# A two-branch layer (state-space scan and gated FFN) on one core: a new order of all queues, earlier gate and phases, lane swap by DMA, and dummy matmuls first

## The chip, the cores and the metric

The kernel runs on one core of one Trainium2 chip. The metric is the device time of the kernel in microseconds (us). The profiled span, from the first to the last instruction, is about 1.7 us shorter than the time. Five engines matter: TensorE (PE, the matmuls; PEld its weight loads), VectorE (DVE), ScalarE (ACT), GpSimd (POOL) and the queue engine SP, which issues most of the DMA transfers. Each engine works through its own instructions in program order and waits on semaphores for the others. PSUM is the memory that the matmuls write, divided into banks; an eviction is the copy of a finished bank to another memory, and the bank can be written again only after it. The granted clock is the share of its full speed that TensorE was given.

## The reference, cut to what matters

```python
# x: (1, 2048, 448) bf16;  P = D = 448;  F = 1792
g = sigmoid((x * gate_w).sum(-1, keepdims=True))           # one number per row
# branch a: diagonal complex state space
Lam_bar = exp(dt * Lam);  B_bar = ((Lam_bar - 1) / Lam)[:, None] * B
h[t] = Lam_bar * h[t-1] + B_bar @ x[t]                      # 2048 steps
a = 2 * real(C @ h) + x * Dskip
# branch b: FFN
b = silu(x @ w1) @ w2
out = g * a + (1 - g) * b
```

## The kernel before

Two time steps are folded into one, so the scan has 1024 steps. `XT` holds x transposed, its even and odd rows one above the other. The parts that count here:

- `ffn1(c, fb)`: 4 matmuls of 512 columns, evicted by ScalarE with silu. There are four passes `c` of 14 blocks. `ffn2(c, q)`: 14 matmuls of 448 columns, evicted by ScalarE with the gate as scale.
- `bu(m, h)`: 7 matmuls of 512 columns for the scan's input, row block `m` of 8, evicted by ScalarE into `HS`.
- tables: the scan is done in a rotating frame. For each of 4 lane groups VectorE computes a phase (3 operations of 128x1024) and ScalarE makes sine and cosine of it.
- `scan(pt)`: VectorE rotates, runs the recurrence, and rotates back into `HS`.
- `ytile`: 8 matmuls `HS` x `C` plus 4 for the direct part; VectorE mixes it with the FFN result. `k0`: 28 matmuls for the direct part, from `CO`.
- The last lane group has only 64 complex lanes. They are packed, real parts in the upper and imaginary parts in the lower half of block 6. A rotation needs the other half as well, so the kernel computes block 7, the same lanes swapped, by matmul.

Their order before (cut; `side` is a generator of VectorE and ScalarE work, `pump` runs a piece of it):

```python
side = chain(side_params(), side_tables(0), side_coef(), side_diag(), side_C(True),
             side_tables(1), side_gate(), side_tables(2), side_tables(3), side_C(False))
for _ in range(2):
    next(side)                      # parameters and tables(0) stand AHEAD of all FFN1
for c in range(2):
    for fb in range(NFB):
        ffn1(c, fb)
        pump()                      # tables 1..3 and the gate between FFN1's evictions
for pt in range(3):
    ...                             # bu of two blocks, then scan(pt)
... bu(6), bu(7), rest of side, scan(3), k0
ffn2(0) x4; ffn1(2); ffn2(1) x4; ffn1(3); ffn2(2) x4
ffn2(3, q), ytile, store ...

def side_tables(pt):
    X, RR = G[:, 0, :], G[:, 1, :]  # ONE shared buffer: phase pt+1 waits for ScalarE's tables of pt
    ...
def side_gate():
    for kt in range(NKT):
        s = kt % 2
        ld("sp", OT[s][:, :], x2[kt * 128:(kt + 1) * 128, :], f"OT{s}_0")   # two small buffers
        ...                         # two products with row sums
```

## Time and profile before

| | before |
|---|---|
| time, median of 3 runs | 215.34 us (214.61 to 218.18) |
| profiled span | 213.8 us |
| PE busy | 163.9 us (77%) |
| DVE busy | 114.1 us (53%) |
| mean granted TensorE clock | 0.894 |

A run more than 1.5% above the fastest of its kernel, as 218.18 us is here, counts as slow.

The first view is the page's second part for the kernel before: the span in 40 equal slices of 5.3 us, each digit the busy share in tenths; PEclk is the granted TensorE clock.

```profile
...
PE   0550009939703349999999999999999999999994
...
DVE  0439999903567696499999999700000021213332
...
PEclk9997556975985557999999999999999999999999
...
```

From slice 16 (about 80 us) PE is full to the end. Ahead of that it holds little work and, having been idle, drops to half clock (the fives). So the loss lies in the first 80 us.

The second view is the list of waits of PE in the kernel before (who waited for whom: total us, times, longest), and the third the timeline of PE (start, length, what, and in brackets the idle time ahead of it with what ended it).

```profile
...
PE ps L493 <- ACT AT L498: 37.9, 5, 17.6
...
```

```profile
...
12.23 1.89 PE L493 MATMUL ps<-XT,W1E 128*128 128x512 bf16 x8 [0.51 <-DMA W1E<-in_B_w_dram]
31.68 11.47 PE L493 MATMUL ps<-XT,W1E 128*128 128x512 bf16 x43 [17.55 <-ACT AT L498]
46.81 10.70 PE L493 MATMUL ps<-XT,W1E 128*128 128x512 bf16 x35 [3.66 <-ACT AT L498]
66.51 1.89 PE L493 MATMUL ps<-XT,W1E 128*128 128x512 bf16 x4 [9.01 <-ACT AT L498]
72.66 1.89 PE L493 MATMUL ps<-XT,W1E 128*128 128x512 bf16 x4 [4.26 <-ACT AT L498]
77.93 3.59 PE L493 MATMUL ps<-XT,W1E 128*128 128x512 bf16 x8 [3.39 <-ACT AT L498]
81.32 18.98 PE L528 MATMUL ps<-XT,LT 128*128 128x512 bf16 x81
```

PE waits 37.9 us for `AT` evictions: four PSUM banks are full, and ScalarE, whose queue is in order, is itself standing at a sine table. What it stands for shows in the chain of waits (start, length, what), a piece of it:

```profile
...
61.90 2.50 DMA OT<-in_A_x_dram
...
67.67 1.24 DVE G L380
...
68.94 1.06 ACT SIN L382
...
76.25 1.15 ACT COS L385
77.39 0.49 ACT AT L498
...
77.93 3.59 PE ps L493 x8
81.53 7.12 PE ps L528 x29
...
```

Gate load, gate, phase, sine, absolute value, cosine, the next phase, its tables, and only then an FFN1 eviction, 8 last FFN1 matmuls at half clock (3.59 us, 449 ns each), and Bu.

### The profile page before, as it was taken

The page shows a single profiled execution, that of the slowest core. Times are in us where ns is not written, and L with a number is a line of the kernel's source. Part 1 is how long each engine was busy: PE and PEld are TensorE (multiplying, and loading weights), DVE is VectorE, ACT ScalarE, POOL GpSimd, SP SyncE. Part 2 cuts the span into 40 slices and gives each one's busy share as a digit, 9 for nine tenths or more (in the row PEclk, how much of TensorE's full clock was granted, in tenths as well). Part 3 has the DMA queues.
Part 4 walks back from the last instruction along what each step waited for, and adds up shares of the span by engine and source line. Part 5 has one row for each costly group of instructions (what it writes and reads, how often), then busy time and mean ns, then how long its engine had stood idle before and what let it go on. Part 6 is the DMA issues. An engine that isn't in the chain of part 4 may idle for free.

```text
span 213.8 us, 2064 instructions
## 1 busy us (share of the span) xinstructions
PE 163.9 (77%) x784; PEld 77.2 (36%) x792; DVE 114.1 (53%) x212; ACT 71.3 (33%) x112; POOL 7.3 (3%) x16
## 2 busy tenths in 40 slices
PE   0550009939703349999999999999999999999994
PEld 0210003403300013444455544454445555555552
DVE  0439999903567696499999999700000021213332
ACT  0500095393102682434332277325642201110000
POOL 7500000000000000000000000000000000000000
PEclk9997556975985557999999999999999999999999
DMA  6998498795440000000000000000000001111111
GB/s 141 351 295 156 88 168 156 209 335 210 129 129 2 0 0 0 0 0 2 3 0 0 0 3 0 0 0 0 3 0 0 0 3 43 43 43 46 43 55 73
DMA packets 27363, 14.58 MB, mean 68 GB/s; under 512 B 20885, under 2 KB 26458, under 8 KB 27354
## 3 DMA queue, kind: packets, MB, share of 16 engines
q1 hardware_dynamic: 26384, 12.85, 23.5%
q10 hardware_dynamic: 970, 1.61, 2.2%
q8 instruction: 6, 0.10, 0.2%
q14 instruction: 3, 0.02, 0.0%
HBM read 8.03 MB, written 1.84 MB: 46 GB/s over the span
## 4 chain that ended last, share of the span: by engine, by line
PE 62%; DVE 15%; DMA 11%; SPq 7%; ACT 3%; issue 1%; DVEq 0%
PE ps L511 20%; PE ps L493 13%; PE ps L528 12%; PE ps L610 11%; DMA OT<-in_A_x_dram 8%; SPq L208 4%; SPq L205 3%; DVE JK L457 3%; PE ps L621 3%; DMA Y<-in_A_B_re_dram 3%; PE ps L543 3%; DVE TMP L340 2%; DVE BB L342 2%; DVE G L380 2%; ACT COS L385 1%
## 5 line engine op out<-in xcount | busy, mean ns | idle before, releaser
L493 PE MATMUL ps<-XT,W1E 128*128 128x512 bf16 x110 | 34.8, 482 | 38.5 <-ACT AT L498 37.9
L629 DVE SCALAR_TENSOR_TENSOR OT<-ps,GT,LT 128x448 bf16<-128x448 f32 x16 | 10.9, 684 | 62.5 <-PE ps L621 54.3
L511 PE MATMUL ps<-W,AT 128*128 128x448 bf16 x224 | 43.4, 352 | 0.0
L498 ACT ACTIVATE AT<-ps 128x512 bf16<-128x512 f32 x56 | 32.4, 596 | 15.6 <-PE ps L493 15.6
L493 PEld LDWEIGHTS ps<-XT,W1E 128*128 128x128 bf16 x112 | 12.5, 117 | 59.9 <-ACT AT L498 42.0
L511 PEld LDWEIGHTS ps<-W,AT 128*128 128x128 bf16 x224 | 21.7, 98 | 20.0 <-issue 0.2
L528 PE MATMUL ps<-XT,LT 128*128 128x512 bf16 x110 | 25.1, 389 | 0.1
L516 ACT ACTIVATE LT<-ps,GT 128x448 bf16<-128x448 f32 x16 | 10.1, 633 | 44.5 <-PE ps L511 44.5
L493 PE MATMUL ps<-XT,W1O 128*128 128x512 bf16 x108 | 24.0, 379 | 0.2
L457 DVE SCALAR_TENSOR_TENSOR JK<-OT,GWB 128x448 bf16<-128x448 bf16 x16 | 10.0, 625 | 12.5 <-DMA OT<-in_A_x_dram 11.9
L528 PEld LDWEIGHTS ps<-XT,LT 128*128 128x128 bf16 x112 | 11.3, 101 | 14.2 <-issue 1.7
L564 DVE TENSOR_TENSOR_SCAN G<-P,Q 128x1024 f32<-128x1024 f32 x7 | 15.7, 2278 | 0.0
L493 PEld LDWEIGHTS ps<-XT,W1O 128*128 128x128 bf16 x112 | 11.0, 98 | 13.1
L532 ACT ACTIVATE HS<-ps 128x512 bf16<-128x512 f32 x16 | 9.6, 597 | 15.5 <-PE ps L528 15.5
L610 PE MATMUL ps<-CE,HS 128*128 128x448 bf16 x64 | 13.4, 352 | 0.0
L610 PE MATMUL ps<-CO,HS 128*128 128x448 bf16 x64 | 13.4, 352 | 0.0
L382 ACT ACTIVATE SIN<-G 128x1024 bf16<-128x1024 f32 x4 | 4.2, 1056 | 22.4 <-DVE G L380 22.4
L610 PEld LDWEIGHTS ps<-CO,HS 128*128 128x128 bf16 x64 | 6.3, 98 | 5.8
L610 PEld LDWEIGHTS ps<-CE,HS 128*128 128x128 bf16 x64 | 6.1, 98 | 5.1
L340 DVE TENSOR_SCALAR TMP<-XC,P 128x448 f32<-128x448 bf16 x16 | 7.2, 453 | 0.5
L621 PE MATMUL ps<-KT,XT 128*128 128x448 bf16 x32 | 7.4, 352 | 0.0
L561 DVE TENSOR_TENSOR Q<-G,SIN 128x1024 bf16<-128x1024 f32 x6 | 7.3, 1219 | 0.0
(69 smaller groups left out, 112.0 us busy)
## 6 DMA issues: line engine op xcount, KB each, us to landing
OT<-in_A_x_dram SPq DMA_DIRECT2D x8, 224.0 KB, 2.5
out_dram<-OT SPq DMA_DIRECT2D x8, 224.0 KB, 1.9
W<-in_B_w_dram SPq DMA_DIRECT2D x1, 1568.0 KB, 8.2
W1O<-in_B_w_dram SPq DMA_DIRECT2D x1, 1344.0 KB, 10.7
W1E<-in_B_w_dram ACTq DMA_DIRECT2D x1, 1152.0 KB, 7.1
W1E<-in_B_w_dram ACTq DMA_DIRECT2D x2, 192.0 KB, 5.8
BB<-in_A_B_re_dram SPq DMA_DIRECT2D x1, 336.0 KB, 6.8
BB<-in_A_B_im_dram SPq DMA_DIRECT2D x1, 336.0 KB, 7.1
```

The lines of the kernel that those rows point to most:

```text
L340: T.op("dve", lambda e: e.tensor_scalar(TMP[:, :], y, ys, None, ALU.mult), reads=reads, writes=["TMP"])
L457: T.op("dve", lambda e, s=s, i=i, kt=kt: e.scalar_tensor_tensor(JK[:, :], OT[s][:, i * D:(i + 1) * D], 1.0, GWB[:, i * D:(i + 1) * D], ALU ...
L493: ins = pe.matmul(ps[:, bank, :], W[:, j, fb * 128:(fb + 1) * 128], XT[:, j0 + j, h * 512:(h + 1) * 512], start=(j == 0), stop=(j == 3))
L498: T.op("act", lambda e: e.activation(a[:, fb, :], ps[:, bank, :], AF.Silu), reads=[f"ps{bank}"], writes=[f"AT{c % 2}_{fb}"])
L511: ins = pe.matmul(ps[:, bank, 0:D], a[:, fb, q * 128:(q + 1) * 128], W2[:, fb, :], start=(fb == 0), stop=(fb == NFB - 1))
L516: T.op("act", lambda e: e.activation(bs(tile), ps[:, bank, 0:D], AF.Copy, scale=GT[:, 2, tile:tile + 1]), reads=[f"ps{bank}", "GT2"], writ ...
L528: ins = pe.matmul(ps[:, bank, :], LT[:, m, j, :], XT[:, j, h * 512:(h + 1) * 512], start=(j == 0), stop=(j == 6))
L532: T.op("act", lambda e: e.activation(HS[:, m, 8 + h * 512:8 + (h + 1) * 512], ps[:, bank, :], AF.Copy), reads=[f"ps{bank}"], writes=[f"U{m ...
L564: T.op("dve", lambda e: e.tensor_tensor_scan(G[:, c, :], rb, Q1[:, c, :], 0.0, ALU.mult, ALU.add), reads=[f"Q1{c}", "rr"], writes=[f"G{c}"])
L610: ins = pe.matmul(ps[:, bank, 0:D], HS[:, m, o0:o0 + 128], C[:, m, :], start=(m == 0), stop=False)
L621: ins = pe.matmul(ps[:, bank, 0:D], XT[:, j, t0:t0 + 128], KT[:, j, :], start=False, stop=(j == 3))
L629: T.op("dve", lambda e: e.scalar_tensor_tensor(o[:, odd * D:(odd + 1) * D], ps[:, bank, 0:D], GT[:, 1, tile:tile + 1], bs(tile), ALU.mult, ...
```

## The change

Intent: give PE work from the first microseconds on and put everything of VectorE and ScalarE next to it. Its parts:

1. Order of PE: FFN1 pass 0, Bu of blocks 0, 1, 6, FFN1 pass 1, Bu of 2 to 5, then FFN2 and FFN1 by turns, k0, y. ScalarE's tables are put between evictions at chosen places.
2. Phases of all four groups are computed early, each into the part of `HS` that its Bu product fills later, so no phase waits for a table. The gate comes before the scans, from one load of x into the still unused `W1O`.
3. The swapped lanes are made by DMA (a swap of halves of `HS` before and of a product after the scan), so `bu(7)` and the eighth products of y go.
4. Twelve dummy matmuls ahead of the first real one, to raise the clock.
5. Smaller: lincombs in pairs through two temporaries, activation tables loaded ahead, FFN2, Bu, k0 and y share four PSUM banks.

```diff
+        def warm(n):                       # n matmuls of zeros into a bank nobody reads
+            ...
+        warm(9)
+        T.op("pe", mm_cols, ...)
+        warm(3)
 ...
+        def phase(pt):
+            return HS[:, 2 * pt:2 * pt + 2, :].rearrange("p a b -> p (a b)")[:, 0:2 * NK].bitcast(F32)
 ...
+        XN = W1O[:, :, :].rearrange("p a b -> p (a b)")
+        def load_xn():
+            ld("sp", XN.rearrange("p (k c) -> p k c", k=NKT), x2.rearrange("(k p) c -> p k c", p=128), "XN")
 ...
+                T.dma("sp", lambda e: e.dma_start(u[0:64, 1, :], u[64:128, 0, :]), ...)     # scan(3)
+                T.dma("sp", lambda e: e.dma_start(u[64:128, 1, :], u[0:64, 0, :]), ...)
 ...
+                T.dma("sp", lambda e: e.dma_start(Q2[0:64, 1, :], Q2[64:128, 0, :]), ...)
+                T.dma("sp", lambda e: e.dma_start(Q2[64:128, 1, :], Q2[0:64, 0, :]), ...)
 ...
-                for m in range(8):         # ytile
+                for m in range(7):
 ...
+        for fb in range(NFB):
+            ffn1(0, fb)
+            if fb in (8, 10, 12):
+                run(tabs, 1)               # tables of groups 0 and 3
+        for h in range(2):
+            for c in range(2):
+                bu(c, h)
+                run(tabs, 1)
+        bu(6, 0)
+        bu(6, 1)
+        load_w2()
+        run(gates, 5)
+        s3 = scan(3)
+        run(s3, 1)
+        for fb in range(NFB):
+            ffn1(1, fb)
+            if fb % 3 == 2:
+                run(tabs, 1)               # tables of groups 1 and 2
+        run(gates)
+        run(s3, 1)
+        run(coef, 1)
+        run(s3)
+        load_c()
+        run(scan(0))
+        ... bu(2), bu(3), scan(1), bu(4), bu(5), scan(2)
+        ... ffn2(0), ffn1(2), ffn2(1), run(coef) (diagonals, CO, CE), ffn1(3), ffn2(2), k0
```

## The prediction

> **What bounds the kernel now.** Span 213.8 us (time 215.3, 1.5 more). In the stretch table TensorE (PE) is at 99% from 80 us to the end at clock 1.00, but holds only 31 us of work in the first 80. The chain of waits says why: through 81 us it runs over VectorE (DVE) and queue issues, not PE. B combinations wait for their last load until 14.7; PE's first FFN1 half then waits for evictions that stand behind ScalarE's sine tables, and those behind DVE's phases (PE idle 17.6 us before 31.7, then 3.7); the gate's x loads come through two buffers (9.4 us, then about 2.5 each); the last tables run one at a time (66 to 77). Idle PE also falls to clock 0.50 (427 instead of 216 ns per 512-column matmul).
>
> From 81.5 on everything is PE work. So all PE work at full clock is: FFN1 224x0.2165 = 48.5, Bu 112x0.2165 = 24.2, FFN2 42.4, k0 5.6, y 24.2+6.1+1.5: about 153 us. About 60 us are lost, nearly all before 81.
>
> **What the change does.** PE work: lane swap by DMA removes one of eight Bu and one of eight y products: -3.0 and -3.0, leaving about 147. Order: FFN1 waits for no table; phases go to unused HS space; gate loads come as one transfer; Bu alternates with FFN1; the tables fill ScalarE gaps. Dummy matmuls (12x0.43, before the data) pay the half-clock start: the trace's first 8 real matmuls took 432 ns, the next 8 236. The Trainium skill, "TensorE: Matmul & The Clock Gate", Part 1, states full rate after about 3.4 us busy; 8.3 to 12 us here agrees.
>
> DVE gets no slack: work is 114 us, about 4 less without CE7, CO7 and BB copies' waits. Added: copies, one 0.69 add, one less 1.2 product.
>
> **PE schedule I expect:** FFN1 starts 8.5 to 9 (loads), first half ends 22; Bu0,1,6 to 31; FFN1 to 43; Bu2-5 to 55; FFN2/FFN1/FFN2/FFN1/FFN2 to 111; k0 to 117; then 39.4 (trace: 6.63 and 3.98 per tile pair, less 0.38) to 156; last eviction and store 3: span 159 unstalled.
>
> **DVE schedule:** parameters to 9.6, B and phases to about 28.6; idle until the 1.8 MB x load (issued about 27, W2 took 8.2 us for 1.6 MB) at 35; gate 10.7 to 46; scan 3 and coefficients to 56; swap wait; three scans of 14.2 to 100-103; diagonals, CO to 112, CE to 120. y needs CE at about 119, k0 needs CO at 111: DVE and PE finish nearly together, so each DVE delay after 28 us shows one for one. I expect scan 3's second swap to stand behind the 1.6 MB W1O load (10.7 us landing before) on the same queue, costing DVE some 3 us; "DMA: Bandwidth & Descriptors", on HWDGE ordering, states ring order per engine; no trace here shows it yet. With 1 to 2 us of start stalls: span about 162.5, time **164.0 us**, 8 in 10 between **158.5 and 174.0**. Faster by over 2%: 0.98; within: 0.01; slower: 0.01.
>
> **What would show it.** PE busy at least 9 tenths in nearly every slice from 9 us; Bu matmuls 216 ns; no wait of FFN1 for evictions above 2 us; DVE idle about 6 us before the gate, about 3 before scan 3's last add; k0 or first y waiting on CO/CE 0 to 4 us.
>
> **What would make it wrong.** Start loads in a new order contending (FFN1 starting after 11); x landing after 38, so that Tanh blocks Bu evictions and everything slips; DVE finishing CE past 125; PE clock lost at an early gap.

## The result, and the profile after

| | before | after |
|---|---|---|
| time, median | 214.98 us (4 runs) | 164.28 us (163.36 to 164.53, 4 runs) |
| ratio, fast runs | | 0.764 (95%: 0.760 to 0.768) |
| profiled span | 213.8 us | 162.8 us |
| PE busy | 163.9 us (77%) | 154.5 us (95%) |
| DVE busy | 114.1 us | 109.8 us |
| mean granted clock | 0.894 | 0.977 |

A ratio here is the mean time of one kernel's fast runs over that of the other's of the same rounds, so it is not quite the ratio of the medians. The forecast was 164.0 us.

The same slices (now 4.1 us each) for the kernel after:

```profile
...
PE   6549999999999999999999999999999999999992
...
DVE  0559999306999999999999999999401131133342
...
PEclk9955999999999999999999999999999999999999
...
```

PE is full from the fourth slice on; its first real work begins in the third, at 10.2 us, and what the first two hold are the dummies. The clock stands at half in slices 3 and 4, in spite of those dummies. VectorE, nearly as full as PE from slice 4 to slice 28, has one empty slice there, the ninth: its wait for the x load. The chain of waits of the kernel after is nearly PE alone; its first large pieces and the first of the y phase:

```profile
...
2.66 7.29 DMA W1E<-in_B_w_dram
...
10.20 14.85 PE ps L530 x56
25.05 9.06 PE ps L564 x42
34.11 12.09 PE ps L530 x56
46.20 12.09 PE ps L564 x56
58.29 10.59 PE ps L548 x56
...
103.93 10.59 PE ps L548 x56
114.53 1.32 PE ps L579 x7
...
120.14 2.75 PE ps L548 x14
...
```

Before 10.20 us it is queue issues and one load, the first FFN1 weights. The first pass of 56 FFN1 matmuls takes 14.85 us, the second 12.09: 2.76 us lost to half clock. Everything else is at full clock without a gap: 2x10.59 us for 112 matmuls of 448 columns is 189 ns each.

The waits of PE, and then those of DVE, in the kernel after:

```profile
...
PE ps L530 <- DMA W1E<-in_B_w_dram: 3.3, 1, 3.3
...
```

```profile
...
DVE JK L487 <- DMA W1O<-in_A_x_dram: 8.2, 1, 8.2
...
DVE HS L597 <- DMA Q<-Q: 0.2, 1, 0.2
```

The 37.9 us of waits for evictions are gone. VectorE waits 8.2 us for the one large x load, and 0.2 us for the swap. Two lines of VectorE's timeline show how early `CO` and `CE` are ready (the last instruction of each):

```profile
...
108.36 0.69 DVE L378 SCALAR_TENSOR_TENSOR CO<-XC,P,TMP 128x448 bf16<-128x448 bf16 x1
...
115.19 0.68 DVE L378 SCALAR_TENSOR_TENSOR CE<-XC,P,TMP 128x448 bf16<-128x448 bf16 x1
```

`CO` is done at 109.05 and k0 starts at 114.53; `CE` is done at 115.87 and y needs it at 122.9. So by this reading VectorE has 5.5 and 7 us in hand, where the prediction gave it none. About half of the difference is PE being late and not VectorE being early: the prediction had k0 at 111 and y at 119.

Where did 51 us go? The span falls by 51.0. Of PE's waits for evictions 37.9 us vanished; PE's busy time fell by 9.4 us, of which the trace gives 6.06 to the products that went (14 of 512 and 16 of 448 columns at 216.5 and 189 ns); the rest of it, with the dummies added, is less time at half clock. The remaining 3.7 us are mostly an earlier start: PE's waits ahead of its first work and weights were 8.0 + 0.5 us and are 1.3 + 0.6 + 3.3.

### The profile page after: what moved, and what is told of

It reads as the page before. It is cut to its first block, busy times and chain, and to the rows that moved or that the text cites. A ratio compares the mean times of both kernels' runs of the same rounds, so it can differ in the third digit from the quotient of the medians.

```text
span 162.8 us, 2017 instructions
## 1 busy us (share of the span) xinstructions
PE 154.5 (95%) x774; PEld 74.4 (46%) x774; DVE 109.8 (67%) x216; ACT 67.8 (42%) x111; POOL 7.3 (4%) x16
## 4 chain that ended last, share of the span: by engine, by line
PE 92%; DMA 4%; ACTq 1%; DVE 0%; issue 0%
PE ps L530 31%; PE ps L548 26%; PE ps L659 13%; PE ps L564 13%; DMA W1E<-in_B_w_dram 4%; PE ps L670 4%; PE ps L579 3%; ACTq L204 1%; PE ps L666 1%; DVE OT L678 0%; PE ps L662 0%; PE ps L581 0%; PE ps L464 0%
## 5 line engine op out<-in xcount | busy, mean ns | idle before, releaser
L535 ACT ACTIVATE AT<-ps 128x512 bf16<-128x512 f32 x56 | 32.7, 597 | 15.8 <-PE ps L530 15.7
L530 PE MATMUL ps<-XT,W1E 128*128 128x512 bf16 x112 | 27.1, 407 | 3.3 <-DMA W1E<-in_B_w_dram 3.3
L564 PE MATMUL ps<-XT,LT 128*128 128x512 bf16 x98 | 21.5, 379 | 0.0
L530 PEld LDWEIGHTS ps<-XT,W1E 128*128 128x128 bf16 x112 | 11.5, 103 | 18.8 <-issue 7.3
L600 DVE TENSOR_TENSOR_SCAN G<-P,Q 128x1024 f32<-128x1024 f32 x7 | 15.7, 2277 | 0.0
L564 PEld LDWEIGHTS ps<-XT,LT 128*128 128x128 bf16 x98 | 9.6, 98 | 11.6
L487 DVE SCALAR_TENSOR_TENSOR JK<-W1O,GWB 128x448 bf16<-128x448 bf16 x16 | 8.8, 622 | 8.2 <-DMA W1O<-in_A_x_dram 8.2
L659 PE MATMUL ps<-CO,HS 128*128 128x448 bf16 x56 | 11.9, 352 | 0.0
L659 PE MATMUL ps<-CE,HS 128*128 128x448 bf16 x56 | 11.9, 352 | 0.0
L568 ACT ACTIVATE HS<-ps 128x512 bf16<-128x512 f32 x14 | 8.4, 598 | 6.8 <-PE ps L564 6.6
L597 DVE TENSOR_TENSOR Q<-G,SIN 128x1024 bf16<-128x1024 f32 x7 | 8.5, 1218 | 0.0
L597 DVE TENSOR_TENSOR Q<-G,COS 128x1024 bf16<-128x1024 f32 x7 | 8.5, 1209 | 0.0
L266 PE MATMUL ps<-Q 128*128 128x512 bf16 x12 | 4.8, 569 | 1.3 <-DVE SG L211 1.3
```

The lines of the kernel that those rows point to most:

```text
L487: T.op("dve", lambda e, t=t: e.scalar_tensor_tensor(JK[:, t % 2, :], XN[:, t * D:(t + 1) * D], 1.0, GWB[:, :], ALU.mult, ALU.mult, accum_o ...
L530: ins = pe.matmul(ps[:, bank, :], W[:, j, fb * 128:(fb + 1) * 128], XT[:, j0 + j, h * 512:(h + 1) * 512], start=(j == 0), stop=(j == 3))
L535: T.op("act", lambda e: e.activation(a[:, fb, :], ps[:, bank, :], AF.Silu), reads=[f"ps{bank}"], writes=[f"AT{c % 2}_{fb}"])
L564: ins = pe.matmul(ps[:, bank, :], LT[:, m, j, :], XT[:, j, h * 512:(h + 1) * 512], start=(j == 0), stop=(j == 6))
L568: T.op("act", lambda e: e.activation(HS[:, m, 8 + h * 512:8 + (h + 1) * 512], ps[:, bank, :], AF.Copy), reads=[f"ps{bank}", f"F{pt}"], wri ...
L597: T.op("dve", lambda e: e.tensor_tensor(o, a, b, op), reads=reads, writes=writes)
```

## The experiments

Runs that were sent together shared one chip. The control, run with the first three, gave 163.55 us, ratio 0.7588. Its first FFN1 matmul started at 9.80 us, and its first FFN1 pass took 13.8 us. Experiments e4 to e6 with e8, and e7 with e9 to e11, ran on two other chips, so they are compared with the control by the ratio to the kernel before.

```profile
...
5.40 1.46 PE L266 MATMUL ps<-Q 128*128 128x512 bf16 x3
9.80 13.93 PE L530 MATMUL ps<-XT,W1E 128*128 128x512 bf16 x55 [2.94 <-DMA W1E<-in_B_w_dram]
23.57 9.23 PE L564 MATMUL ps<-XT,LT 128*128 128x512 bf16 x41
...
```

> The changed kernel itself, as the control on the same chip as the next three. Expected 163.4 to 164.6 us, first FFN1 matmul at about 10.2 us, the clock granted at 0.5 from about 8.7 to 15.5, first FFN1 half 14.9 us.

Start and clock vary from run to run by themselves: between this run and the profile above the start differs by 0.4 us and the first pass by 1 us, and the six runs of the control show mean clocks from 0.976 to 1.0. So the first pass of one profile is not a measure by itself to better than 1 us. Nor is a mean clock of 1.0 proof of full clock: the views are made of the clock changes that the trace records, and ahead of the first of these they show 1.00. In e1 the first recorded change is a rise at 14.15 us, and up to there the matmuls start 0.43 us apart, after it 0.22.

### e1: no dummies

```diff
-        warm(9)
         T.op("pe", mm_cols, ...)
-        warm(3)
```

> All 12 dummy matmuls taken out. Theory A (the dummies do nothing here: the 3.3 us without a matmul before the first weights land lose the clock again): same time as the control within 0.7 us, first FFN1 half again about 14 to 15 us. Rival (they shorten the slow start as the change intends): the first half takes longer than the control's by 1 to 2 us and so does the whole.

Measured: 163.74 us, ratio 0.7597 against 0.7588 of the control; the means of the fast runs are 163.76 and 163.51, so 0.15% apart and within the scatter. The PE timeline of this run:

```profile
...
9.66 14.45 PE L528 MATMUL ps<-XT,W1E 128*128 128x512 bf16 x55 [3.54 <-DMA W1E<-in_B_w_dram]
23.94 9.23 PE L562 MATMUL ps<-XT,LT 128*128 128x512 bf16 x41
...
```

The first pass takes 14.3 us here. As shipped, the dummies are worth nothing that shows. Theory A holds so far as that; why is for the next run.

### e2: dummies up to the data

```diff
-        warm(3)
+        warm(18)
```

> 18 instead of 3 dummies behind the parameter columns, so that they reach to about 10 us, where the first weights land. Theory A: the clock stays at 1.0, the first FFN1 half takes 12.1 us instead of 14.9, and the time falls by 2.3 to 2.9 us to about 161.6. Rival (the half rate comes from something else, such as the load of weights or a fixed start phase): no gain, or up to 0.5 us lost since the dummies overrun the data.

Measured: 161.97 us (161.75 to 162.22), ratio 0.7512, clock 1.0 in every run; its mean is 1.6 us or 1.0% below the control's. PE timeline:

```profile
...
5.04 4.06 PE L266 MATMUL ps<-Q 128*128 128x512 bf16 x18
10.28 12.27 PE L530 MATMUL ps<-XT,W1E 128*128 128x512 bf16 x55 [1.18 <-DMA W1E<-in_B_w_dram]
22.38 9.43 PE L564 MATMUL ps<-XT,LT 128*128 128x512 bf16 x41
...
```

The idle gap ahead of the data is 1.2 us instead of 2.9 to 3.3, and the pass takes 12.1 us. So reaching nearly to the data is worth 1.6 us. The run changes two things at once, the gap and the number of dummies, and the recorded clock changes suggest that both count. Twelve dummies are only just enough to raise the clock: it rose at 5.26 us in the profile after and at 6.78 in the control, and not before 13.29 in e3, which has the same twelve. Where it rose, it fell again at 8.67 and 10.19, within the gap or at its end. Here it rose at 4.02 and stayed. What in the gap decides is taken up under e11. The gain is 1.6 and not 2.3 to 2.9, because the control's own first pass lost only 1.7 us to half clock in its profiled run (13.8 against 12.1), and the data came 0.5 us later here. This version beats both kernels.

### e3: a smaller first block of weights

```diff
-        ld("act", W1E[:, 0:3, 0:512], ...); ld("act", W1E[:, 0:3, 512:], ...)
+        for k, a, b in (("W1Eb", 0, 256), ("W1Ed", 256, 768), ("W1Ec", 768, F_FF)):
+            ld("act", W1E[:, 0:3, a:b], ...)
```

> The first block of FFN1 weights cut from 512 to 256 columns (then 512, then the rest). If the first FFN1 matmul waits only for bytes ahead of it in the queue, it starts 1.0 to 1.6 us earlier (about 8.8 us) and the gap shrinks to 1.9 us. Theory A then also predicts that the clock is held or nearly so: time 160.5 to 163. If the gap is still long enough to lose the clock, only the earlier start is gained: about 163.

Measured: 163.13 us, ratio 0.7571: same as the control within the scatter. The load of half the bytes took as long (192 KB landed 7.1 us after issue; the 384 KB of the control took 6.9), and the first FFN1 matmul started at 9.98. The theory of bytes ahead in the queue fell for this load. The gap was 2.5 us and the first pass took 13.7; this run can't tell whether such a gap loses the clock, since here the dummies had not raised it.

### e4: the lanes by matmul again

```diff
-        (two swaps by DMA in scan(3))
+                tt(HS[:, 6, H0:], G[:, 0, :], cs, ...); tt(HS[:, 7, H0:], G[:, 0, :], sn, ...)
-                for m in range(7):   # ytile
+                for m in range(8):
+            bu(7, h) after bu(6, h);  LT7, C7 and their coefficients as before the change
```

> The lane swap put back on the matmul engine inside the new order (an eighth Bu product, an eighth y product, an eighth C pair, no swap by DMA). Theory (after 10 us only the sum of matmul work counts): 14 matmuls of 512 and 16 of 448 columns return, +3.0 and +3.0 us: 169.0 to 170.2 us. Rival (the swap by DMA costs nearly as much in waits as it saves): 164 to 167.

Measured: 170.65 us, ratio 0.7919, that is 7.1 us over the control if both ratios are taken of 215.3. Of it, 6.06 us are the matmuls; the trace shows 0.81 us more, a wait of the small diagonal product for a ScalarE eviction, since two more Bu products shift the rotation of the banks. The swap by DMA gives back what it takes off PE and costs nothing that shows.

### e5 and e6: VectorE delayed

```diff
         load_c()
+        for _ in range(3):     # e6: range(8); 1.22 us each, result unused
+            T.op("dve", lambda e: e.tensor_tensor(G[:, 1, :], IOTA[:, :], IOTA[:, :], ALU.subtract), ...)
         run(scan(0))
```

> Three idle 1.22 us products (3.7 us) on VectorE before the first scan. The recorded prediction said VectorE and the matmul engine finish nearly together, so each delay shows one for one: +3.7, about 167.5. The trace of the changed kernel says CO is ready 5.4 us before k0 needs it and CE 6.8 us before y: +0, about 163.6.

> Eight such products (9.8 us). One for one: about 173.4. With the slack of 5.4 us before k0 read from the trace: +4.3, about 168 (k0 then waits for CO).

Measured: e5 164.3 us, ratio 0.7621, and PE waits for nothing but its first weights; its interval (0.7586 to 0.7656) holds the control's 0.7588. 3.7 us of delay are free to within the scatter (0.7 us), and the one-for-one claim is refuted. e6 took 171.01 us, ratio 0.7934, 7.4 us over the control, where the slack read off k0 said 4.3. Its PE waits and timeline:

```profile
...
PE ps L548 <- DVE PV L468: 5.5, 1, 5.5
...
```

```profile
...
102.09 2.81 PE L548 MATMUL ps<-W,AT 128*128 128x448 bf16 x14
110.38 10.45 PE L548 MATMUL ps<-W,AT 128*128 128x448 bf16 x42 [5.47 <-DVE PV L468]
120.66 1.49 PE L579 MATMUL ps<-CO,BB 128*128 128x448 bf16 x7
...
```

The wait came up at another place: not at k0, but in the third FFN2, which needs a PSUM bank that VectorE's copy of the diagonals (`PV`, line 468) still holds. The bank was wanted at 104.9 and the copy came at 110.2. The real slack is thus about 4.3 us (9.8 minus 5.5), at that copy. And the idle 5.5 us cost the clock once more: the 42 matmuls after it took 10.28 us up to the start of k0, where 42x0.189 = 7.94 is the full rate. Wait 5.5 plus clock 2.3 makes the 7.4 with a little to spare.

### e7: the gate through two buffers again

```diff
-        load_xn()                                    # one load of 1.8 MB
+                if t % 2 == 0:
+                    ld("sp", OT[(t // 2) % 2][:, :], x2[...], ...)   # 8 loads of 224 KB, two buffers
-        load_w2()
         run(gates, 5); s3 = scan(3); run(s3, 1)
+        load_w2()
```

> The changed kernel with its gate loads through two small buffers again, as in the kernel before, at the new early place. Theory (VectorE has about 4 us of slack after the gate and waits 8 us for the one large load anyway): gate starts earlier, about 32, ends about 47 as now; time within 1 us of the control's 163.6. Rival (the single load is part of the gain): the two-buffer waits of about 2.5 us per pair and the swap standing behind them cost over 2 us.

Measured: 163.18 us, ratio 0.7562: nothing lost. VectorE's waits in it:

```profile
...
DVE JK L490 <- DMA OT<-in_A_x_dram: 5.6, 5, 1.4
...
```

The single load of the change is not part of the gain that shows: the gate starts at 31.8 instead of 38.1 and ends its last product at 45.2 instead of 46.8. Load size was not what the gate needed; that its early place was is not shown by a run of its own. This run also tells about the swap (its first two transfers of 128 KB): with no large load just ahead of them in the queue they took 2.7 us to land; in the kernel after, behind W2 of 1.6 MB, 6.8 us.

### e8 and e9: the order alone, in the kernel before

e8 takes the kernel before and changes only the place of its calls; e9 mends one spot of e8.

```diff
+        for fb in range(NFB): ffn1(0, fb)
+        pump(12)                              # params, tables(0), coefficients, diagonals, CO
+        for fb in range(NFB): ffn1(1, fb)
+        # e8: pump(1) (tables(1)); all bu; rest of side; four scans; k0; then as before
+        # e9: tables(1..3) ahead of the gate, one each ahead of Bu of 0-1, 2-3, 4-5; bu 6, 7;
+        #     rest of side; four scans; k0 only after the third FFN2
```

> The kernel before with nothing but its order changed: first FFN1 half before any table, then the first tables, the second half, all Bu, then gate, tables and scans on VectorE beside FFN2 and FFN1; no dummies, lanes by matmul, gate loads through two buffers, phases in the shared buffer. Theory (the 60 us lost were PE waiting in program order behind a VectorE chain that itself could run beside later matmul work): VectorE ends its scans at about 133, y starts at 134, end near 177: time 175 to 182, so about 37 of the 51 us. Rival (the early gate and phases are what matters, order alone is held by VectorE all the same): over 195.

> The order alone again, with the spot mended that the first such run showed (k0's evictions behind the last tables on ScalarE, 10 us of idle PE and then half clock): all tables before the gate, between the Bu groups, and k0 after the third FFN2. Nothing else of the change. Expected: Bu ends about 68, FFN2 may wait 2 to 5 us for the gate, y starts near 137, end near 178: 176 to 184 us. If it stays above 187, order alone gives only half of the 51 us and the early phases and gate are needed for the rest.

Measured: e8 191.05 us, ratio 0.8883, outside the expected 175 to 182 and below the rival's 195. Its trace shows PE idle for 9.9 us at k0, whose evictions I had put behind the last two tables in ScalarE's queue, and half clock after it. e9 gave 182.17 us, ratio 0.8436, inside the expected 176 to 184. PE timeline of e9:

```profile
...
30.68 11.63 PE L493 MATMUL ps<-XT,W1E 128*128 128x512 bf16 x39 [3.93 <-ACT AT L498]
...
47.33 6.20 PE L528 MATMUL ps<-XT,LT 128*128 128x512 bf16 x27 [2.00 <-ACT HS L532]
54.76 6.22 PE L528 MATMUL ps<-XT,LT 128*128 128x512 bf16 x28 [1.22 <-ACT HS L532]
62.20 9.24 PE L528 MATMUL ps<-XT,LT 128*128 128x512 bf16 x41 [1.22 <-ACT HS L532]
71.27 10.76 PE L511 MATMUL ps<-W,AT 128*128 128x448 bf16 x56
...
```

So order alone is worth 33.7 us of 215.6 (1 minus 0.8436), about two thirds of the gain; e8 and e9 differ by 9 us through the place of a few calls. What e9 still lacks against the kernel after (182.2 against about 163.6) is 18.6 us. Experiment e4 gives 6 to 7 us of that to the lanes. The waits that e9's timeline shows for ScalarE, 3.93 + 2.00 + 1.22 + 1.22 = 8.4 us, are those that early phases in their own memory take away; some 2.6 us of half clock follow the first of them (11.5 us from 30.68 to Bu at 42.15 for 41 matmuls, of which two records are missing; 41x0.2165 is 8.9). The profiled runs alone differ by 15.9 us (178.7 against 162.8): 6.06 + 8.4 + 2.6, less 1.4 for e9's first FFN1 matmul, at 8.79 instead of 10.20, makes 15.7. That this remainder is due to the phases is read off the trace and was not tested by a run with the phases alone.

### e10 and e11: trying to start earlier

e10: ten dummies behind the columns, meant to reach the data (they ended 2.1 us short), and the tail row block of the weights cut to its first 512 columns as well. e11: the same, and B's two loads moved behind the weights.

```diff
+        warm(10)                                           # instead of 3
-        ld("act", W1E[0:64, 3, :], B_w1[384:448, :], "W1Ea")
+        ld("act", W1E[0:64, 3, 0:512], B_w1[384:448, 0:512], "W1Ea")
+        ...                                                # the other 1280 columns after the first block
 e11:
-        ld("sp", BB[...], A_B_re...); ld("sp", BB[...], A_B_im...)
+        ld("act", BB[...], A_B_re...); ld("act", BB[...], A_B_im...)   # after all W1E loads
```

> Dummies up to the data (10 behind the columns) and the fourth row block of the FFN1 weights also cut to its first 512 columns (160 KB fewer ahead of the first product). If the load that ends last is held by bytes ahead of it in its queue, the first FFN1 matmul starts 0.5 to 1.2 us earlier than 10.2 and the time is 160.8 to 161.6; the run with dummies alone was 162.0. If the engines are simply shared with the other queue, 161.6 to 162.3.

> As the run before, and the two loads of B move from the other queue to stand behind the FFN1 weights. If the early matmul is held by sharing the engines with B (0.67 MB), it starts at 8.3 to 9.3 and the time is 160 to 161; B lands about 2 us later, which VectorE's 8 us wait before the gate should swallow. If VectorE's later start shows after all, no gain or a loss of up to 2 us.

Measured: e10 169.63 us (0.7838), 5.4 us slower than the control by the ratios, and slow in all its runs (167.9 to 171.0); two of its six were over 1.5% above the fastest, so they are left out of the ratio. e11 164.17 us (0.7618; one slow run of six, 167.82, left out), no gain. PE timelines of e10, then e11:

```profile
...
10.23 3.61 PE L531 MATMUL ps<-XT,W1E 128*128 128x512 bf16 x16 [2.10 <-DMA W1E<-in_B_w_dram]
19.54 10.64 PE L531 MATMUL ps<-XT,W1E 128*128 128x512 bf16 x39 [5.70 <-issue]
...
```

```profile
...
5.08 2.33 PE L267 MATMUL ps<-Q 128*128 128x512 bf16 x10
9.82 13.07 PE L531 MATMUL ps<-XT,W1E 128*128 128x512 bf16 x51 [2.41 <-DMA W1E<-in_B_w_dram]
...
```

Neither start moved: 10.23 and 9.82. In e10 the rest of the weights landed 15.6 us after issue instead of 10.2 (control), so PE stopped for 5.7 us after four blocks; the transposing loads of x took longer too (median 7.3 us to landing, against 5.1), but so they did in e11 (7.1). Why the same bytes, cut in two, slow the whole start phase down is open: e11 has the same cut, and its weights landed after 10.7 us. So the cut alone does not do it. What holds the first weights at 9.6 to 10.0 us is open as well; three ways of taking bytes off did not move it. e11 has a side result: its gap after the dummies was 2.4 us, and the clock was still lost (0.50 from 12 to 14 us in the stretch table, while the first matmuls after the gap ran at full rate).

That leads to what in a gap loses the clock. Its length alone does not decide: e11's 2.4 us lost it, and the 2.1 us of e10 with the same 19 dummies and the 2.34 us that e8's PE waits ahead of 46.92 did not. In all 14 traces the recorded clock changes are multiples of 3.41 us apart. Cut each trace at that step from its first change: every stretch of 3.41 us that began at full clock and in which PE was idle for 2.13 us or more ended with the fall to half (e11's from 7.69 to 11.10 holds 2.13), and every one with 1.86 us or less of idle time kept the full clock (e10's gap falls into two stretches, with 1.5 and 0.6 us; e8's likewise, with 0.97 and 1.37; e2's lies in one, with 1.18). This is read from the traces kept, with no run made to test it.

## Why the prediction was right or wrong, point by point

The forecast, 164.0 us, met 164.28. Part of this is luck: two terms of the sum were off and cancelled, the half clock (2.8 us instead of none) and the wait for VectorE (none instead of about 2).

- "About 60 us are lost, nearly all before 81", and the sum of PE work near 147 us: right. The chain after shows 149.5 us of PE from 10.20 to 159.67, of which 2.76 are half clock, so 146.7 of work. The largest part of the gain is order (e9: 33.7 us).
- "Lane swap by DMA removes ... -3.0 and -3.0": right (e4: +7.1, of which 6.06 matmuls and 0.81 a bank wait).
- "Dummy matmuls pay the half-clock start": this step failed. I took the Trainium skill's "TensorE: Matmul & The Clock Gate", Part 1, for the rise of the clock and left out of the sum that it need not last over the gap to the data, although I placed that data at 8.5 to 9 us and had only 12x0.43 = 5.2 us of dummies; "PE clock lost at an early gap" stands only in the list of what would make the prediction wrong. The same page's section "HAM oscillation" warns of idle gaps over about 3.4 us; the gap here was 3.3 us in the profile after and 2.9 in the control, so that figure would not have warned me. e1 (no dummies: no change) and e2 (dummies nearly to the data: -1.6 us) settle that the step failed. The term was 2.76 us in the profiled run.
- "FFN1 starts 8.5 to 9", with 1 to 2 us for start stalls: it started at 10.2, so it fits only with that allowance used up.
- "Each DVE delay after 28 us shows one for one", CE at 120, k0 or y waiting 0 to 4 us: this step failed. CE was ready at 115.9 and nothing waited. I had costed lincombs (linear combinations, two VectorE operations each) at about 1.14 us; in pairs they take 0.96 (1.91 a pair in the timeline after, against 1.21 for a single one before), and the 16 gate products, which now write two buffers by turns, 0.55 instead of 0.67 (that the buffers are the cause was not tested). The other part is PE: it came to k0 and to y 3.5 and 3.9 us later than planned. e5 shows 3.7 us of delay to be free; e6 puts the slack at about 4.3 us, held by a PSUM bank and not by CO or CE.
- "Scan 3's second swap ... costing DVE some 3 us": wrong in size, 0.2 us. The swap did stand behind another load (6.8 us for the first swap against 2.7 in e7), which fits "DMA: Bandwidth & Descriptors", on HWDGE ordering (of the DMAs that SP and ScalarE issue: descriptors of one engine's ring are consumed in order). But VectorE had 3.1 us of coefficient work to do meanwhile (54.1 to 57.2), so next to nothing of it showed.
- "x landing at 35", "DVE idle about 6 us": 38.1 and 8.2 us. The prediction feared a landing after 38; it did no harm (PE waits for no eviction after 10.20, and in e7 a gate that starts 6 us earlier changes nothing).

So the sum should have read: start 10.2, work 146.7, half clock 2.8, end 3.1, VectorE 0: 162.8. Mine was start 8.5 to 9 plus 1 to 2, work 147, half clock 0, end 3, and about 2 left for VectorE, the middle of its 0 to 4.

## What to carry to other kernels

When one engine's work, summed at its full rate, is far below the span, look first at the place of calls in the in-order queues of the others: one table ahead of an eviction can hold PSUM banks and so the matmuls, and moving calls alone gave two thirds of this gain. Dummy matmuls paid here only when they both raised the clock and reached nearly to the data (e1, e2); check in the trace when the clock rose and how long PE idles after the last of them. Measure slack by delaying an engine on purpose: it shows not only how much there is, but at which wait, which here was another than the one that reading the profile named.

## What the Trainium skill lacked or had wrong

- "TensorE: Matmul & The Clock Gate", section "Why this matters for your kernels" ("No PE-idle gaps >~3µs between matmul bursts"): shorter gaps cost the clock here too. After 12 and 19 dummies gaps of 2.9 us (control) and 2.4 us (e11) lost it; gaps of 1.2 us (e2), 2.1 us (e10) and 2.34 us (e8) kept it. The page's free-running window, 3.4 us in Part 1, fits: the changes lie multiples of 3.41 us apart, and in e11 the drop comes 1.3 us after the real matmuls had begun. But the page calls for a whole window of idle, and 2.13 us of idle in one was enough (e11), while 1.86 us was not (e8).
- Part 1 of the same page ("Seeing it yourself") warns that the clock's trace events can be unreliable; no trace here shows that: in e0, e1, e2 and e11 the spacing of the matmuls changes within one matmul of each recorded change. What no page has is that nothing is recorded ahead of the first change, so that the views show 1.00 there: in e1 the stretch table has 1.00 from 10 to 14 us, while only 3 or 4 matmuls of 512 columns start in each microsecond (at full rate it would be 4.6). The matmuls' spacing is what to read at the start of a kernel.
- "DMA: Bandwidth & Descriptors" gives no way to foresee when a small load lands in a start phase with transposing loads on the other queue: 192, 384 and 384 KB (e3, control, e10) landed 7.1, 6.9 and 7.3 us after issue, and cutting 160 KB off the head of the queue slowed the whole by 5.4 us in e10 and did not in e11, where B's loads had moved as well. No page that I read has this.
